# Cluster masks from cluster numbers through crossbar DMA transposes, in a routed-attention kernel with an expert router behind it

## The chip, the cores and the metric

The kernel runs on one core of one Trainium2 chip, in one launch. The metric is device time in microseconds (us), the median of the runs shown. Nothing is computed on the host.

## The reference: what is computed

The first half is attention that is restricted to clusters. Each query and each key is given to the centroid (16 for each head) with which it has the largest cosine, and a query sees only the keys of its own cluster:

```
q_assign = argmax(q_n @ c_n.T)          # 16 centroids for each head
k_assign = argmax(k_n @ c_n.T)
mask     = q_assign[..., :, None] == k_assign[..., None, :]
scores   = where(mask, scale * q @ k.T, -1e9)
attn     = softmax(scores);  out = attn @ v     # 4 batches, 8 heads, 768 rows, 64 columns
```

The second half takes the attention output as 3072 tokens of 512 values, gives each token to one of 8 experts by its cosine with the expert's embedding, and computes `gate * (relu(x @ w1[e]) @ w2[e])` with w1 of 512x1024 and w2 of 1024x512 for each expert. All is float32.

## The kernel before

**Tiling.** The attention is worked in 16 pairs: a pair is one batch and two heads (`pairs`), whose 2x64 columns fill 128 partitions. A pair has 12 units: two halves of the queries (`hq`, 384 columns each) times six blocks of 128 keys (`j`). Six units of the same half are a group, whose sums share one accumulator. For a unit, `scores` (L361) puts the scores transposed, keys on partitions, into a PSUM tile of two banks, one for each head; `expo` (L377) lets ScalarE (ACT) take the exponential into `prob`; `attend` (L382) multiplies it with v into `o_ps` and lets VectorE (DVE) add it to `acc`, the group's denominators before they are summed over partitions. `total` (L411) sums `acc` over partitions with a matmul, and DVE inverts it; `divide` (L427) scales the output; `rows` (L443) turns it back to rows.

**The mask.** It is added inside the score product. Each token has a one-hot row of its cluster, 16 columns and one column of +1 or -1, padded to 64 for each head; the product of the key's and the query's rows, the latter times 2**60, is 0 for the same cluster and -2**60 for another. So the first two matmuls of a unit (L369, bf16, K = 64 rows for each head) lay down the mask, and two float32 products add the scores.

**How a pair's masks are made** (`prep_pieces`, L238), one pair ahead of its use. `turn0` and `turn1` (L260) turn q and k, loaded in 32x32 blocks, with a DVE block transpose. `products` (L264): four matmuls with the centroids, copied out by ACT (`asT`, L276). `assign` (L278): three float32 transposes on TensorE (PE) bring tokens back on partitions (L281), DVE takes the maximum and compares (L289, L290), GpSimd (POOL) multiplies with 16 ... 1 so that ties go to the first cluster (L291). `choose` (L293): DVE's maximum `pm` (L297) is the cluster's number, and a compare with it writes the one-hot tile `oh` (L298). `turn_hot` (L305): 12 bf16 transposes on PE for q and k (L311), evicted by DVE as `qH` (L317) and by ACT as `kH` (L320). `values` (L323) adds up v on POOL, and `mean` (L332) turns that sum into a column `ev` that `divide` uses.

**The order of the work** is written out by hand for PE, DVE and ACT, which run their instructions in exactly the order of the program; POOL and SP (the queue that issues the loads) follow the order that the framework's scheduler chose. The main loop (L861) takes two units at a time; I call such a step an iteration, six of them (`it` 0 to 5) to a pair. In each, PE gets the scores of the *next* two units, then the pieces that `between` (L812) deals out, then the attend products of the present two units, and at `it` 0 and 3 the `total` of the group just finished:

```
it 0: turn1(n+1)      it 1: values, products(n+1), rows   it 2: assign(n+1), rows
it 3: choose(n+1)     it 4: hots(n+1)                     it 5: turn0(n+2)
```

Because scores run one iteration ahead, the first scores of pair n+1, and with them its masks, are asked for at the start of `it` 5 of pair n. The loads of v for pair n+1 are issued in `it` 0 and those of q and k for pair n+2 in `it` 1, all on SP. In pair 1 four loads of expert weights, 2 MB each, are issued as well (L870, L873). Pools: `prob` has five buffers (`pp`), `s_ps` two, the PSUM tile `misc` two, the masks two (`trp`).

**After the attention** (from about 408 us on) 28 blocks of 128 tokens go through the experts. The change touches nothing there.

Of the kernel before, what the change touches and what calls it, by code (L numbers as in the profile page):

```python
# [9 lines left out]
F32 = mybir.dt.float32  # L10
BF16 = mybir.dt.bfloat16
# [28 lines left out]
def kernel(  # L40
# [44 lines left out]
    w2s = [const.tile([P, KF, DM], F32, name=f"w2s{i}") for i in range(2)]  # L85

    ident = const.tile([P, P], F32, name="ident")
    identb = const.tile([P, P], BF16, name="identb")
    cnB = const.tile([P, NHP, 2 * C], F32, name="cnB")
    embT = const.tile([P, KD, 2 * C], F32, name="embT")  # L90
    prefc = const.tile([P, C], BF16, name="prefc")
# [74 lines left out]


    make_identity(nc, ident)
    make_identity(nc, identb)
    make_upper_triangular(nc, sltb, val=1.0, diag=False)  # L170
    nc.vector.memset(onesb, 1.0)
    nc.vector.memset(ones, 1.0)
# [22 lines left out]
    nc.vector.tensor_scalar(tok_t, tok_i, 6, None, ALU.arith_shift_right)  # L195
    nc.vector.tensor_scalar(tok_hi, tok_t, 1, None, ALU.add)

    ohs = [const.tile([P, NJ // 2, 4, 2, D], BF16, name=f"oh{i}") for i in range(2)]
    for oh in ohs:
        nc.gpsimd.memset(oh, 0.0)  # L200
        for t in range(2):
            nc.gpsimd.memset(oh[:, :, 2 * t : 2 * t + 2, :, C : C + 1], (-1.0, 1.0)[t])

    def unit_rows(dst, src, n):

# [32 lines left out]
    def prep_pieces(n):  # L238

        hp = pairs[n][1]  # L240
        t = ld[n]
        oh = ohs[n % 2]

        def turn(nm, half):
            if half == 0:
# [18 lines left out]
        def products():  # L264

            bk = misc()
            for i in range(4):
                nc.tensor.matmul(  # L268
                    bk[2 * C * i : 2 * C * i + 2 * C, 0:HS],
                    lhsT=cnB[:, hp],  # L270
                    rhs=t["qk"[i // 2] + "T"][:, HS * (i % 2) : HS * (i % 2) + HS],
                    start=True,
                    stop=True,
                )
            t["asT"] = smp.tile([P, HS], F32, tag="asT", name="asT", bufs=1)
            nc.scalar.copy(t["asT"], bk[:, 0:HS])  # L276

        def assign():  # L278
            bk = misc()
            for u in range(NJ // 2):  # L280
                nc.tensor.transpose(  # L281
                    bk[:, P * u : P * u + P], t["asT"][:, P * u : P * u + P], ident
                )
            shp = [P, 4 * NJ, C]
            asn = bk[:, 0 : 4 * NJ * C].rearrange("p (g c) -> p g c", c=C)
            amax = smp.tile(shp[0:2], F32, tag="amax", name="amax")
            sel = smp.tile(shp, BF16, tag="sel", name="sel", bufs=1)
            t["sel"] = sel
            nc.vector.tensor_reduce(amax, asn, axis=AXX, op=ALU.max)  # L289
            nc.vector.tensor_tensor(sel, asn, bc(amax, shp, 2), ALU.is_equal)  # L290
            nc.gpsimd.tensor_tensor(sel, sel, bc(prefc, shp, 1), ALU.mult)  # L291

        def choose():  # L293

            shp = [P, 4 * NJ, C]
            pm = smp.tile(shp[0:2], BF16, tag="pm", name="pm")
            nc.vector.tensor_reduce(pm, t["sel"], axis=AXX, op=ALU.max)  # L297
            nc.vector.tensor_tensor(  # L298
                oh.rearrange("p u t h c -> p (u t h) c")[:, :, 0:C],
                t["sel"],  # L300
                bc(pm, shp, 2),
                ALU.is_equal,
            )

        def turn_hot(i, nm):  # L305
            hot = t[nm + "H"] = trp.tile([P, S], BF16, tag=nm + "H", name=nm + "H")
            bank = misc()
            bk = bank.bitcast(BF16)
            for j in range(NJ):
                half, u = divmod(j, NJ // 2)  # L310
                nc.tensor.transpose(  # L311
                    bk[:, P * j : P * j + P],
                    oh[:, u, 2 * i + half].rearrange("p h c -> p (h c)"),
                    identb,
                )
            if nm == "q":
                nc.vector.tensor_scalar(hot, bk[:, 0:S], BIG, None, ALU.mult)  # L317
            else:
                mean(bank)
                nc.scalar.copy(hot, bk[:, 0:S])  # L320
                nc.vector.tensor_copy(t["ev"], bank[:, HS : HS + 1])

        def values():  # L323

# [7 lines left out]
        def mean(bk):  # L332

            nc.tensor.matmul(
                bk[:, HS : HS + 1],
                lhsT=t["vs"][:, 0].rearrange("p h d -> p (h d)"),
                rhs=epsc,
                start=True,
                stop=True,
            )  # L340
            t["ev"] = smp.tile([P, 1], F32, tag="ev", name="ev")

        return {
            "turn0": lambda: turn_blocks("q") if n else (turn("q", 0), turn("k", 0)),
# [2 lines left out]
            "products": products,  # L347
            "assign": assign,
            "choose": choose,
            "hots": lambda: (turn_hot(0, "q"), turn_hot(1, "k")),  # L350
        }


# [7 lines left out]
    def scores(i):  # L361

        n, hq, j = units[i]
        t = ld[n]
        s_ps = un[i]["s_ps"] = psS.tile([P, 2, 512], F32, tag="s_ps", name="s_ps")
        for l, r, first in (("kH", "qH", True), ("kT", "qT", False)):
            for h in range(2):
                rows = slice(D * h, D * h + D)
                nc.tensor.matmul(  # L369
                    s_ps[:, h, 0:HS],  # L370
                    lhsT=t[l][rows, P * j : P * j + P],
                    rhs=t[r][rows, HS * hq : HS * hq + HS],
                    start=first,
                    stop=not first,
                )

    def expo(i):  # L377
# [4 lines left out]
    def attend(i):  # L382

        n, hq, j = units[i]
        d, g = un[i], gr[i // GU]
        if j == 0:
            g["o_ps"] = psO.tile([P, 512], F32, tag="o_ps", name="o_ps")
        for h in range(2):
            nc.tensor.matmul(  # L389
                g["o_ps"][D * h : D * h + D, 0:HS],  # L390
                lhsT=ld[n]["v"][:, j, h],
                rhs=d["prob"][:, h],
                start=(j == 0),
                stop=(j == NJ - 1),
            )
        if j == 1:
            g["acc"] = xp.tile([P, 2, HS], F32, tag="acc", name="acc")
            nc.vector.scalar_tensor_tensor(  # L398
                out=g["acc"],
                in0=un[i - 1]["prob"],  # L400
                scalar=NJ * EPS,
                in1=d["prob"],
                op0=ALU.add,
                op1=ALU.add,
            )
            un[i - 1].clear()
        elif j > 1:
            nc.vector.tensor_tensor(g["acc"], g["acc"], d["prob"], ALU.add)  # L408
            d.clear()

    def total(g):  # L411

        d = gr[g]
        bk = misc()
        for h in range(2):
            nc.tensor.matmul(  # L416
                bk[D * h : D * h + D, 0:HS],
# [385 lines left out]
        (3, 3): lambda: (pa.tokens(), fetch(0), fetch(1), fetch(2)),  # L803
    }

    def piece(n, name):
        if n < NP:
            if n not in prepare:
                prepare[n] = prep_pieces(n)
            prepare[n][name]()  # L810

    def between(n, it):  # L812
        b, nb = divmod(n, NHP)
# [16 lines left out]
                rows(2 * n - 1)  # L830
        elif it == 3:
            piece(n + 1, "choose")
        elif it == 4:
            piece(n + 1, "hots")
        if b > 0:
            if nb == 0 and it == 3:
                route[b - 1] = route_pieces(b - 1)
# [14 lines left out]
            weights(1)  # L852

    with tc.manual_schedule(engines={EngineType.PE, EngineType.DVE, EngineType.Activation}):
        for name in ("turn0", "turn1", "values", "products", "assign", "choose", "hots"):
            piece(0, name)
        load(1, "qk")
        for m in range(2):
# [150 lines left out]
```

## Time and profile before

| | |
|---|---|
| median of three runs | 842.67 us (839.86 to 843.57) |
| the profiled execution | 841.56 us, its span 839.8 us |
| attention stage, first scores to last attend product | 21.95 to 407.9 us |
| one pair, from one v load's issue to the next (190.46 to 213.74) | 23.3 us |
| mean of the 12 pairs from 71.85 to 358.6 us | 23.9 us |
| VectorE busy between 180 and 210 us | 26.35 of 30 us |
| ScalarE, GpSimd in the same 30 us | 17.13 and 3.76 us |

The span is the time between the first and the last instruction on the core, and the 1.8 us between it and the execution's own time lie outside of the records. The page shows busy time for each engine; a busy PE means that matmuls overlap without a hole, each with its pipeline's fill and drain in its duration, so what a matmul costs is read from the distance between starts. "PEld" is the load of stationary weights, "SPq" the issue of a DMA on the SP queue. A group's line names the tile that is written, an arrow, and the tiles that are read.

### The profile page before, as it was taken

What the parts mean: (1) busy time and instruction counts of PE and PEld (TensorE: products, weight loads), DVE (VectorE), ACT (ScalarE), POOL (GpSimd) and SP (SyncE); (2) the same over time, 40 slices, a digit from 0 to 9 for tenths busy, and PEclk for the clock granted to TensorE, in tenths of its full rate; (3) what the DMA queues carried; (4) which work ended last, traced back from release to release, by engine and by line L of the source; (5) the groups of instructions that cost most, each with busy time, mean ns of one, the idle gap of its engine ahead of it and who ended that gap; (6) DMA issues with size and microseconds to landing.
All of it is one profiled execution on the core that took longest, in us unless ns stands there. A gap on an engine that the chain in (4) does not pass through costs nothing.

```text
span 839.8 us, 12523 instructions
## 1 busy us (share of the span) xinstructions
PE 806.9 (96%) x5047; PEld 474.3 (56%) x5047; DVE 372.1 (44%) x521; ACT 293.9 (35%) x459; POOL 126.9 (15%) x172
## 2 busy tenths in 40 slices
PE   4999999999999999998997999999999999999995
PEld 2444444444444444443685667676776768676672
DVE  3588888898889988898560000000000000000000
ACT  2555556755576556754431111111111111111110
POOL 4011110211111111220120111110101011010100
PEclk9999999999999999999998999999999999999998
DMA  9269552284343721040279449566574838126400
GB/s 156 97 242 182 71 62 43 26 132 57 57 58 73 116 47 23 9 95 1 74 169 396 152 146 334 205 220 252 183 289 155 315 130 328 43 93 249 157 29 22
DMA packets 158381, 115.23 MB, mean 137 GB/s; under 512 B 124261, under 2 KB 124261, under 8 KB 158320
## 3 DMA queue, kind: packets, MB, share of 16 engines
q1 hardware_dynamic: 153664, 100.69, 44.8%
q0 software_dynamic: 4480, 13.65, 4.3%
q8 instruction: 42, 0.69, 0.3%
q14 instruction: 19, 0.16, 0.1%
q10 hardware_dynamic: 176, 0.05, 0.0%
HBM read 152.11 MB, written 13.64 MB: 197 GB/s over the span
## 4 chain that ended last, share of the span: by engine, by line
PE 45%; issue 27%; DMA 23%; DVE 2%; SPq 1%; POOL 1%; ACT 0%; POOLq 0%; DVEq 0%
PE s_ps L369 18%; DMA out_dram<-y,sidx 18%; PE o_ps L389 15%; PE misc L416 2%; DMA w1s<-in_moe_w_dram 2%; DMA out_dram<-y,gidx 2%; PE h_ps L753 2%; PE misc L450 2%; PE misc L268 1%; PE misc L311 1%; PE misc L281 1%; SPq L154 1%; PE y_ps L769 1%; DMA q<-in_q_dram 1%; PE misc L472 1%
## 5 line engine op out<-in xcount | busy, mean ns | idle before, releaser
L753 PEld LDWEIGHTS h_ps<-xTm,w1s 128*128 128x128 f32 x1792 | 204.7, 194 | 28.4 <-DVE xTm L741 17.5
L753 PE MATMUL h_ps<-xTm,w1s 128*128 128x128 f32 x1792 | 210.2, 278 | 7.0 <-DMA w1s<-in_moe_w_dram 7.0
L769 PE MATMUL y_ps<-w2s,hT 128*128 128x512 f32 x448 | 201.1, 592 | 0.0
L380 ACT ACTIVATE prob<-s_ps 128x768 f32<-128x768 f32 x192 | 153.8, 810 | 121.0 <-PE s_ps L369 112.7
L741 DVE COPY xTm<-x_ps 128x512 f32<-128x512 f32 x24 | 16.6, 692 | 332.1 <-PE x_ps L739 332.1
L369 PE MATMUL s_ps<-qT,kT 64*128 64x384 f32 x768 | 157.6, 489 | 0.0
L389 PE MATMUL o_ps<-prob,v 128*64 128x384 f32 x768 | 145.1, 499 | 0.0
L408 DVE TENSOR_TENSOR acc<-acc,prob 128x768 f32<-128x768 f32 x128 | 129.4, 1011 | 3.5
L769 PEld LDWEIGHTS y_ps<-w2s,hT 128*128 128x128 f32 x448 | 81.0, 190 | 81.8 <-issue 81.8
L760 ACT ACTIVATE hT<-h_ps 128x512 f32<-128x512 f32 x56 | 33.4, 597 | 207.7 <-PE h_ps L753 207.7
L425 DVE RECIPROCAL den<-den 128x384 f32<-128x384 f32 x32 | 81.6, 2551 | 27.2 <-ACT den L424 27.2
L389 PEld LDWEIGHTS o_ps<-prob,v 128*64 128x64 f32 x768 | 46.6, 136 | 64.9 <-issue 56.9
L369 PEld LDWEIGHTS s_ps<-qT,kT 64*128 64x128 f32 x768 | 69.9, 192 | 22.1 <-issue 22.1
L779 ACT ACTIVATE y<-y_ps,xin 128x512 f32<-128x512 f32 x28 | 19.2, 687 | 150.3 <-PE y_ps L769 139.1
L780 POOL DMA_INDIRECT out_dram<-y,sidx x24 | 24.0, 1000 | 291.2 <-ACT y L779 285.3
L369 PE MATMUL s_ps<-qH,kH 64*128 64x384 bf16 x384 | 64.4, 332 | 1.0 <-ACT kH L320 0.9
L369 PEld LDWEIGHTS <-kH 64*128 64x128 bf16 x384 | 19.0, 94 | 71.6 <-issue 48.9
L327 POOL TENSOR_TENSOR vs<-v 128x384 f32<-128x384 f32 x16 | 16.8, 1049 | 198.7 <-DMA v<-in_v_dram 158.6
L291 POOL TENSOR_TENSOR sel<-sel,prefc 128x384 bf16<-128x384 bf16 x16 | 24.2, 1516 | 91.5 <-DVE sel L290 91.5
L709 POOL DMA_INDIRECT xin<-x_rows,gidx x28 | 29.7, 1059 | 41.1 <-issue 19.7
L398 DVE SCALAR_TENSOR_TENSOR acc<-prob 128x768 f32<-128x768 f32 x32 | 30.0, 936 | 3.1 <-ACT prob L380 3.1
L416 PE MATMUL misc<-acc,ones 128*64 128x384 f32 x128 | 26.6, 493 | 3.0 <-DVE acc L408 3.0
(185 smaller groups left out, 437.4 us busy)
## 6 DMA issues: line engine op xcount, KB each, us to landing
w1s<-in_moe_w_dram SPq DMA_DIRECT2D x30, 2048.0 KB
w2s<-in_moe_w_dram SPq DMA_DIRECT2D x30, 2048.0 KB
x_rows<-xr SPq DMA_DIRECT2D x4, 1539.0 KB
v<-in_v_dram SPq DMA_DIRECT2D x32, 192.0 KB
q<-in_q_dram SPq DMA_DIRECT2D x60, 96.0 KB
k<-in_k_dram SPq DMA_DIRECT2D x60, 96.0 KB
xin<-x_rows,gidx POOLq DMA_INDIRECT x28, 7.2
q<-in_q_dram SPq DMA_DIRECT2D x2, 192.0 KB
```

The costliest lines, as they stand in the source:

```text
L291: nc.gpsimd.tensor_tensor(sel, sel, bc(prefc, shp, 1), ALU.mult)
L369: nc.tensor.matmul(s_ps[:, h, 0:HS], lhsT=t[l][rows, P * j : P * j + P], rhs=t[r][rows, HS * hq : HS * hq + HS], start=first, stop=not first,)
L380: nc.scalar.activation(d["prob"], d["s_ps"][:, :, 0:HS], ACTF.Exp, scale=scale)
L389: nc.tensor.matmul(g["o_ps"][D * h : D * h + D, 0:HS], lhsT=ld[n]["v"][:, j, h], rhs=d["prob"][:, h], start=(j == 0), stop=(j == NJ - 1),)
L398: nc.vector.scalar_tensor_tensor(out=g["acc"], in0=un[i - 1]["prob"], scalar=NJ * EPS, in1=d["prob"], op0=ALU.add, op1=ALU.add,)
L408: nc.vector.tensor_tensor(g["acc"], g["acc"], d["prob"], ALU.add)
L416: nc.tensor.matmul(bk[D * h : D * h + D, 0:HS], lhsT=ones, rhs=d["acc"][:, h], start=True, stop=True,)
L425: nc.vector.reciprocal(d["den"], d["den"])
L709: nc.gpsimd.indirect_dma_start(out=xin, out_offset=None, in_=x_rows[0:n], in_offset=bass.IndirectOffsetOnAxis(ap=gidxs[part][:, c : c + 1] ...
L753: nc.tensor.matmul(bk[:, m : m + P], lhsT=w1s[j % 2][:, c, f0 + m : f0 + m + P], rhs=d["xT"][:, P * c : P * c + P], start=(c == 0), stop=( ...
L760: nc.scalar.activation(d["hT"][:, f0 : f0 + 512], bk, ACTF.Relu)
L769: nc.tensor.matmul(bk, lhsT=d["hT"][:, P * c : P * c + P], rhs=w2s[j % 2][:, c], start=(c == 0), stop=(c == KF - 1),)
```

## The change

The one-hot tile and its 12 PE transposes go. In their place each token carries three numbers, its cluster number c, c squared and a constant, so that the product of a key's and a query's three numbers is a constant times (cq - ck) squared. The parts, as the diff has them:

- `products` no longer lets ACT copy the bank; DVE turns it in 32x32 blocks out of PSUM into `asn`. `assign` reads `asn` in SBUF, and its three PE transposes are gone.
- `choose`: after `pm`, POOL writes `cd` (32 tokens by 1536 columns for each of four partition groups; 64 columns for each head of which three are used) with three small operations, and four DMA transposes write the mask tile `hot` (128 by 4 by 384), two of them for the two halves of q, two for those of k. They are issued on SP, for the first pair on ACT's queue. There is one `cd`, where there were two one-hot tiles.
- `hots` is gone from `it` 4. `mean` moves into `total`, in the same PSUM bank, at the end of `it` 3.
- `attend`: at `j` = 1 POOL adds the first two `prob` tiles into `two`; at `j` = 2 DVE adds `two`, the epsilon and the third `prob` (the fused operation that stood at `j` = 1). DVE has one addition fewer for each group.

In the changed kernel's program the four transposes of pair n+1 stand on SP behind the v loads of that pair and most of the q and k loads of pair n+2, in pair 1 behind the four weight loads and all of the q and k loads. On POOL, between the tie-breaking multiply and the three operations on `cd`, stands the `two` of the group that begins at `it` 3. The first scores of a pair wait for the transposes of q's first half, of k's first half, and, being in one queue, of what lies between.

```diff
-    ohs = [const.tile([P, NJ // 2, 4, 2, D], BF16, name=f"oh{i}") for i in range(2)]
-    for oh in ohs:
-        nc.gpsimd.memset(oh, 0.0)
...
+    cd = const.tile([P, S // (2 * SQ), 2, D], BF16, name="cd")
+    wcd = const.tile([P, S // SQ], BF16, name="wcd")
+    nc.gpsimd.memset(cd, 0.0)
+    for i, (p0, w, c) in enumerate(((0, -BIG, BIG / 2), (D, -2.0, 1.0))):
+        g = slice(p0, p0 + D)
+        nc.gpsimd.memset(wcd[g], w)
+        nc.gpsimd.memset(cd[g, :, :, 2 - 2 * i : 3 - 2 * i], c)
...
-            t["asT"] = smp.tile([P, HS], F32, tag="asT", name="asT", bufs=1)
-            nc.scalar.copy(t["asT"], bk[:, 0:HS])
+            t["asn"] = smp.tile([P, HS], F32, tag="asn", name="asn", bufs=1)
+            nc.vector.transpose(t["asn"], bk[:, 0:HS])
 
         def assign():
-            bk = misc()
-            for u in range(NJ // 2):
-                nc.tensor.transpose(
-                    bk[:, P * u : P * u + P], t["asT"][:, P * u : P * u + P], ident
-                )
...
-            nc.vector.tensor_tensor(
-                oh.rearrange("p u t h c -> p (u t h) c")[:, :, 0:C],
-                t["sel"],
-                bc(pm, shp, 2),
-                ALU.is_equal,
-            )
-
-        def turn_hot(i, nm):
...
-            for j in range(NJ):
-                half, u = divmod(j, NJ // 2)
-                nc.tensor.transpose(
...
-            if nm == "q":
-                nc.vector.tensor_scalar(hot, bk[:, 0:S], BIG, None, ALU.mult)
-            else:
-                mean(bank)
-                nc.scalar.copy(hot, bk[:, 0:S])
-                nc.vector.tensor_copy(t["ev"], bank[:, HS : HS + 1])
+            pm, w = (x.rearrange("p (s h) -> p s h", h=2) for x in (pm, wcd))
+            nc.gpsimd.tensor_tensor(cd[..., 1], pm, w, ALU.mult)
+            for i, p0 in enumerate((0, D)):
+                g = slice(p0, p0 + D)
+                nc.gpsimd.tensor_tensor(cd[g, :, :, 2 * i], pm[g], cd[g, :, :, 1], ALU.mult)
+            t["H"] = trp.tile([P, 4, HS], BF16, tag="hot", name="hot")
+            for i in range(4):
+                (nc.sync if n else nc.scalar).dma_start_transpose(
+                    out=t["H"][:, i].rearrange("r (s t) -> r s t", t=SQ),
+                    in_=cd[SQ * i : SQ * i + SQ].rearrange("p s h c -> p (s h c)"),
+                )
...
             t["ev"] = smp.tile([P, 1], F32, tag="ev", name="ev")
+            nc.vector.tensor_copy(t["ev"], bk[:, HS : HS + 1])
...
         if j == 1:
+            d["two"] = xp.tile([P, 2, HS], F32, tag="two", name="two", bufs=1)
+            nc.gpsimd.tensor_tensor(d["two"], un[i - 1]["prob"], d["prob"], ALU.add)
+            un[i - 1].clear()
+        elif j == 2:
             g["acc"] = xp.tile([P, 2, HS], F32, tag="acc", name="acc")
             nc.vector.scalar_tensor_tensor(
                 out=g["acc"],
-                in0=un[i - 1]["prob"],
+                in0=un[i - 1]["two"],
...
-        elif j > 1:
+        elif j > 2:
             nc.vector.tensor_tensor(g["acc"], g["acc"], d["prob"], ALU.add)
...
         bk = misc()
+        if g % 2 == 0:
+            piece(units[GU * g][0] + 1, "mean", bk)
...
-        elif it == 4:
-            piece(n + 1, "hots")
+        elif it == 4 and n == 0:
+            piece(0, "mean", misc())
```

## The prediction

> **What bounds the kernel now.** I read the page's busy times first, then the busy times of 30 us stretches, then the timelines of PE, DVE and POOL over one pair.
>
> ```profile
> 180.00:210.00 30.00, 30.00 (x213) 13.80 (x209) 26.35 (x30) 17.13 (x24) 3.76 (x5) 1.00 0.55 64
> 210.00:240.00 30.00, 30.00 (x213) 13.03 (x209) 25.52 (x30) 17.82 (x29) 3.47 (x4) 1.00 0.26 45
> ```
>
> (PE, PE's weight loads, DVE, ACT, POOL, clock, DMA share, GB/s.) PE has no hole in the attention stage, DVE is at 85 to 88%, POOL at 12%. So PE's order of work is the bound, and each microsecond taken out of it counts, as long as nothing that it waits for becomes late. PE's timeline over `it` 2 (end) to `it` 5 of one pair:
>
> ```profile
> 200.20 0.55 PE L281 MATMUL misc<-ident,asT 128*128 128x128 f32 x3
> 200.58 0.49 PE L450 MATMUL misc<-ident,xT 128*128 128x128 f32 x3
> ...
> 202.45 0.34 PE L369 MATMUL s_ps<-qH,kH 64*128 64x384 bf16 x2
> ...
> 207.98 0.84 PE L311 MATMUL misc<-identb,oh 128*128 128x128 bf16 x12
> 208.66 0.34 PE L334 MATMUL misc<-epsc,vs 128*128 128x1 f32 x2
> 208.92 1.51 PE L389 MATMUL o_ps<-prob,v 128*64 128x384 f32 x8
> 210.36 0.34 PE L369 MATMUL s_ps<-qH,kH 64*128 64x384 bf16 x2
> ```
>
> From start to start the three transposes of L281 take 200.58 - 200.20 = 0.38 us, the twelve of L311 208.66 - 207.98 = 0.68, `mean` 0.26. `it` 3 begins at 202.45, `it` 5, where the next pair's masks are first read, at 210.36. What makes the masks (DVE's rows, then POOL's):
>
> ```profile
> 202.90 1.48 DVE L408 TENSOR_TENSOR acc<-acc,prob 128x768 f32<-128x768 f32 x1
> 204.31 0.54 DVE L297 TENSOR_REDUCE pm<-sel 128x24 bf16<-128x384 bf16 x1
> 204.88 0.56 DVE L298 TENSOR_TENSOR oh<-sel,pm 128x384 bf16<-128x384 bf16 x1
> ```
> ```profile
> 202.01 1.56 POOL L291 TENSOR_TENSOR sel<-sel,prefc 128x384 bf16<-128x384 bf16 x1 [5.28 <-DVE sel L290]
> ```
>
> `pm` is there at 204.85, 2.4 us after `it` 3 began. An addition beside POOL's L291 takes 1.48 us in place of the usual 0.97.
>
> One more place shows what a wait of PE costs, near the end of the stage:
>
> ```profile
> 386.67 1.18 PE L416 MATMUL misc<-acc,ones 128*64 128x384 f32 x4 [2.17 <-DVE acc L408]
> 387.79 0.50 PE L369 MATMUL s_ps<-qH,kH 64*128 64x384 bf16 x2
> 388.08 1.49 PE L369 MATMUL s_ps<-qT,kT 64*128 64x384 f32 x4
> ```
>
> After 2.17 us of idleness the same four matmuls take 1.49 us that take 0.81 elsewhere. From 386.67 to 390.83 PE does what takes 0.74 + 1.72 = 2.46 us in the pair above (205.51 to 206.25, 206.25 to 207.98): a further 1.7 us lost.
>
> **What the Trainium skill says.** (1) "TensorE: Matmul & The Clock Gate", Part 1: PE falls to half its clock after an idle window of some 3.4 us and needs as long to recover. The trace agrees on the slow stretch (some 4 us), but here 2.17 us of idleness was enough. (2) "SBUF — State Buffer", Who interferes with whom: a DVE instruction with two SBUF inputs and a GpSimd instruction that reads SBUF exclude each other for a whole instruction. The trace agrees: 1.48 for 0.97 above, and L291 took 0.91 us alone at the start (at 16.89). (3) "VectorE: DVE Perf Modes", The three transpose paths: a crossbar DMA transpose of 128x128 bf16 is given as 1309 ns. (4) "DMA: Bandwidth & Descriptors", Latency and other measured facts: a fixed cost near 2 us, most of it the receipt of the last bytes, less for targets other than HBM. No crossbar transfer is in this trace; the nearest to (4) is the first load of centroids, issued at 0.75, read by ACT at 3.50, so at most 2.75 us.
>
> **The change part by part**, against the profiled execution's 841.6 us (the median of the runs is 1.1 us above it).
>
> *PE's transposes go*: 0.38 + 0.68 = 1.06 us a pair. Pairs 1 to 15 are prepared beside PE's stream: 15 x 1.06 = -15.9 us. `mean` costs the same 0.26 in its new place; its sum of v was ready at 196.7, 9 us before.
>
> *ACT* loses `asT` (0.48 us) and `kH` (0.80) a pair. ACT waits for PE's scores anyway: nothing.
>
> *DVE* loses `oh` 0.56, `qH` 0.50 and two first additions (2 x 0.94), and gains the transpose of 384 columns out of PSUM, at 0.56 from the nearest row (`amax`, the same read). About 2.4 us less of 21 a pair; DVE isn't the bound, so nothing in the steady pairs. Where it was, at 386.67, it is earlier by one addition for each group; I take 3 of the 2.17 + 1.7 us there as gained: -3.
>
> *POOL's `two`*: 128 columns take 0.45 us and 384 take 1.00 (L328, L327), so 768 take 1.8. Twice a pair, 3.6 us on an engine that is busy for 3; its cost is what stands behind it. In POOL's order the `two` of `it` 3 stands between L291 and the three operations on `cd`. By (2) it shuts out, or is shut out by, DVE's second addition (L408). I take it as getting in after that addition: from 1.9 to 3.7 us after `it` 3's begin. Then three small ones: a chain of six eight-column additions (L514) took 2.23 us, 0.37 each; so 3 x 0.37 = 1.1, and `cd` is ready at 4.8, its first part at 4.5. Bounds: 3.5 if `two` costs nothing, 5.5 if it gets in first and delays `pm`.
>
> *The crossbar transposes*: three must land before `it` 5. That begins 210.36 - 202.45 = 7.9 us after `it` 3 before, less L311's 0.68 = 7.2 after (`mean` only moves). They start at some 4.7. The unknown is the time of one, 96 KB each. Below: the loads of q, k and v in 190 to 200 us are 7680 packets (6144 of 128 B, 1536 of 256 B) at shares 0.47 + 1.18 + 1.51 + 1.36 + 0.06 of 2 us of 16 engines, 19 ns a packet; if a transpose moves 256-byte rows, 384 packets, that is 0.5 us. As 64-byte runs, 1536 packets: 1.8. By (3), three times 128x128: 3.9. I take 0.9 each, near the lower end since sixteen engines share it, and 1.5 us from the last packet to PE: 4.7 + 2.7 + 1.5 = 8.9. **PE then waits 8.9 - 7.2 = 1.7 us in each pair.** Nothing shortens this in the next pair: the chain to `cd` starts from PE's own `total` at `it` 0, which is as late as PE is. Pairs 1 and 3 to 15, 14 of them: 14 x 1.7 = +24. The slow clock after a wait near 2 us costs up to 1.7 more; I take half, since 0.82 us of idleness (before L416 at 74.59) left it at full speed: 14 x 0.85 = +12. Behind the transposes on SP stands only part of k's loads for the pair after, needed 5 us later or more: nothing.
>
> *Pair 2* stands behind four weight loads:
>
> ```profile
> 51.30 17.10 SPq L154 DMA_DIRECT2D q<-in_q_dram  x4
> 68.50 3.24 SPq L154 DMA_DIRECT2D k<-in_k_dram  x4
> ```
>
> These loads are issued only by 71.74, and the transposes come after: landing near 71.7 + 2.7 + 1.5 = 76, where `it` 5 begins at 67: 9 us, and 1.7 for the clock, less 1.05 us (0.23 + 0.82) for which PE stands still there now: +9.
>
> *The first pair*: `asT` and L281 go (the maximum some 1.1 us earlier), and `cd` (1.1) plus three transposes (4.2) stand where L311, `qH`/`kH` took 19.27 to 21.95, less `oh` 0.56: +1.
>
> Sum: -15.9 - 3 + 24 + 12 + 9 + 1 = +27; 841.6 + 27 + 1.1 = **870 us**.
>
> **The rivals.**
> *A, the transposes land in time* (0.4 us each, 1.2 to land: 4.7 + 2.4 = 7.1). Then PE's gain stays: -15.9 - 3 + 1 + 6 for pair 2 = -12: 830 us, faster. For it: the queue is empty from 200 on (share 0.00 in the stretches to 214), SP waits for nothing else. It decides at 0.8 us per transpose with its landing spread over three, that is 2.5 us in all after `cd`. Against: the fixed cost alone nearly uses that up.
> *B, a short wait*, 0.6 us each and 1.3 to land, 7.8: 0.6 x 14 = +8, no slow clock: -15.9 - 3 + 8 + 9 + 1 = -1: 842, no change.
> *C, the crossbar is slow*, 2.5 us each: 4.7 + 7.5 + 1.5 = 13.7, a wait of 6.5 and the slow clock 1.7: 14 x 8.2 = 115; -18.9 + 115 + 13 = +109: 952. For it: the price under (3) scaled by size would be slower still.
> *D, VectorE becomes the bound* through the lock: 21 - 2.4 + 2 x 1.8 = 22.2 us a pair, against PE's 23.3 - 1.06 = 22.2. It would take back the rest of the gain at most: the time is then B's.
>
> **How the numbers follow.** My forecast 0.47 (its own range, with one transpose at 0.7 to 1.3 us, 848 to 905), A 0.23, B and D together 0.12, C 0.18. The range runs from A's middle to C's: 828 to 948. Half a percent, 4 us, is about what a measurement of this kernel can tell from no change. Faster 0.24 (A and a little of B), same 0.09, slower 0.67.
>
> **What would show it.** In PE's timeline after, the bf16 scores of the first unit of each pair carry a wait for a DMA of `hot`, of about 1.7 us, fourteen times, and the float32 scores behind it last 1.5 us in part of the pairs. In POOL's timeline `two` lies between `sel` and the `cd` rows, which end some 4.8 us after `it` 3 begins. Pair 2 shows one wait near 9 us. If PE's rows have no wait for `hot`, A is right and I am wrong; if the wait is over 4 us, C. If PE waits for `acc` and DVE has no idle time, D.

## The result and the profile after

The changed kernel takes 864.11 us (860.88 to 869.56, four runs) against 842.46 us of the kernel before (839.86 to 843.57, four runs): the ratio is 1.0268, with a 95% interval of 1.0208 to 1.0328. The forecast was 870 us, slower, in a range of 828 to 948. The profiled execution took 860.88 us (its span is 859.0), 19.3 us more than the 841.56 of the one before.

The time went into the attention. Its last `total` starts at 432.95 us, before at 411.67: 21.3 us later. What follows, to the end of the span, is 2.1 us shorter (426.05 for 428.13), of which 1.4 are PE's wait for `w1s` (5.6 us for 7.0).

I show the views of the prediction again, now of the kernel after. The two stretches of 30 us (PE, PE's weight loads, DVE, ACT, POOL, clock, DMA share, GB/s):

```profile
180.00:210.00 30.00, 28.05 (x180) 11.59 (x180) 25.40 (x30) 14.34 (x21) 11.17 (x10) 1.00 0.74 122
210.00:240.00 30.00, 28.74 (x189) 11.74 (x187) 23.20 (x23) 14.43 (x21) 10.76 (x12) 1.00 0.50 79
```

PE, which had no hole, is now idle for 1.95 and 1.26 us. POOL works for 11 us instead of 3.5. DVE is idle for longer than before, so VectorE did not become the bound.

PE's timeline from the start of `it` 3 (195.24) to the first masks of the next pair (204.63):

```profile
195.24 0.34 PE L357 MATMUL s_ps<-hot 64*128 64x384 bf16 x2
...
198.40 0.38 PE L316 MATMUL misc<-epsc,vs 128*128 128x1 f32 x2
199.04 0.87 PE L407 MATMUL misc<-acc,ones 128*64 128x384 f32 x4 [0.25 <-DVE ev L324]
...
201.55 1.51 PE L373 MATMUL o_ps<-prob,v 128*64 128x384 f32 x8
204.63 0.34 PE L357 MATMUL s_ps<-hot 64*128 64x384 bf16 x2 [1.57 <-DMA hot<-cd]
204.81 0.81 PE L357 MATMUL s_ps<-qT,kT 64*128 64x384 f32 x4
```

There is the forecast wait for a DMA of `hot`. The float32 scores behind it take 0.81 us, so the clock did not fall. There is also a wait that the prediction did not have: `total` (L407) waits for DVE's copy `ev`. What makes the masks, on POOL, SP and DVE:

```profile
194.28 1.56 POOL L287 TENSOR_TENSOR sel<-sel,prefc 128x384 bf16<-128x384 bf16 x1 [3.74 <-DVE sel L286]
195.81 2.54 POOL L382 TENSOR_TENSOR two<-prob 128x768 f32<-128x768 f32 x1
198.29 0.31 POOL L294 TENSOR_TENSOR cd<-pm,wcd 128x24 bf16<-128x24 bf16 x1
198.68 0.68 POOL L297 TENSOR_TENSOR cd<-pm,cd 64x24 bf16<-64x24 bf16 x2
```
```profile
194.12 2.54 DVE L397 TENSOR_TENSOR acc<-acc,prob 128x768 f32<-128x768 f32 x2
196.58 0.54 DVE L292 TENSOR_REDUCE pm<-sel 128x24 bf16<-128x384 bf16 x1
198.82 0.16 DVE L324 COPY ev<-misc 128x1 f32<-128x1 f32 x1 [1.70 <-PE misc L316]
```
```profile
199.00 5.64 SPq L300 DMA_TRANSPOSE hot<-cd  x4
...
223.41 5.11 SPq L300 DMA_TRANSPOSE hot<-cd  x4
```

`pm` is done at 197.1, but POOL is still at `two`, so the first `cd` operation starts 1.2 us later. `two` takes 1.81 us where nothing disturbs it; here it takes 2.54, because an addition of DVE got in first, which ends at 196.66. Then SP needs 5.11 us for the four transposes where nothing disturbs it, 1.28 for each; the issue of one lasts 1.25 us in the median of 60. PE waits for three. In the set at 199.00 one of them took 1.79 us. In the undisturbed set at 223.41 the third issue ends at 227.2, and PE starts at 228.49, 1.3 us later.

Pair 2, on PE and on SP:

```profile
81.01 0.50 PE L357 MATMUL s_ps<-hot 64*128 64x384 bf16 x2 [11.73 <-DMA hot<-cd]
81.30 1.49 PE L357 MATMUL s_ps<-qT,kT 64*128 64x384 f32 x4
```
```profile
55.94 17.54 SPq L153 DMA_DIRECT2D q<-in_q_dram  x4
73.57 2.18 SPq L153 DMA_DIRECT2D k<-in_k_dram  x4
75.85 5.11 SPq L300 DMA_TRANSPOSE hot<-cd  x4
```

The loads of q and k hold SP until 75.75, and the transposes come after. This wait alone is 11.73 us, and the slow clock behind it 1.8.

The late place near the end of the attention:

```profile
407.95 0.87 PE L407 MATMUL misc<-acc,ones 128*64 128x384 f32 x4 [3.15 <-DVE acc L397]
```
```profile
401.76 1.81 POOL L382 TENSOR_TENSOR two<-prob 128x768 f32<-128x768 f32 x1 [8.12 <-ACT prob L364]
```
```profile
401.94 1.80 DVE L627 TENSOR_TENSOR wa<-wa,eq 128x144 f32<-128x144 f32 x1
```

In the kernel before the same operation of DVE was:

```profile
382.21 0.31 DVE L636 TENSOR_TENSOR wa<-wa,eq 128x144 f32<-128x144 f32 x1
```

The wait there was 2.17 us. It grew, since DVE's small routing operation takes 1.80 us in place of 0.31: it stands beside POOL's `two`, and ends 0.17 us after it.

**Where the 21.3 us are.** I take the distance from one `total` to the next in both traces. The first `total` comes 1.9 us later (the first pair waits for its transposes). The stretch with pair 2's wait is 11.7 us longer, the late place 1.0. The other 28 stretches, two for each of 14 pairs, are 6.7 us longer, 0.48 a pair. In a pair PE has lost 1.06 us of transposes, `mean` costs 0.54 more than before (below), and the 14 waits for `hot` sum to 10.6 us (0 to 1.57 us, mean 0.76). That makes 0.24 of the 0.48; the rest are in part waits for `acc` (named in two stretches, at 259.29 and 356.39, which are 0.4 us longer than mere arithmetic gives: 10.54 for 11.08 - 0.68 - 0.26 = 10.14).

### The profile page after: what moved, and what is told of

Its sections match the earlier page's. It is cut to its first block, busy times and chain, and to the rows that moved or that the text cites. A ratio compares the mean times of both kernels' runs of the same rounds, so it can differ in the third digit from the quotient of the medians.

```text
span 859.0 us, 12213 instructions
## 1 busy us (share of the span) xinstructions
PE 795.8 (93%) x4807; PEld 455.9 (53%) x4807; DVE 355.2 (41%) x473; ACT 274.1 (32%) x427; POOL 208.0 (24%) x249
## 4 chain that ended last, share of the span: by engine, by line
issue 28%; PE 25%; DMA 24%; DVE 12%; SPq 4%; POOL 4%; ACT 2%; ACTq 0%; POOLq 0%; DVEq 0%
DMA out_dram<-y,sidx 17%; PE s_ps L357 10%; PE o_ps L373 7%; DVE den L416 4%; DVE acc L397 3%; DMA hot<-cd 3%; SPq L300 2%; POOL two L382 2%; PE misc L407 2%; DMA w1s<-in_moe_w_dram 2%; DMA out_dram<-y,gidx 2%; PE h_ps L744 2%; SPq L153 1%; DVE acc L386 1%; PE misc L441 1%
## 5 line engine op out<-in xcount | busy, mean ns | idle before, releaser
L397 DVE TENSOR_TENSOR acc<-acc,prob 128x768 f32<-128x768 f32 x96 | 116.9, 1218 | 4.6
L382 POOL TENSOR_TENSOR two<-prob 128x768 f32<-128x768 f32 x32 | 71.0, 2218 | 142.1 <-ACT prob L364 142.1
L357 PE MATMUL s_ps<-hot 64*128 64x384 bf16 x384 | 64.5, 332 | 32.5 <-DMA hot<-cd 32.4
L357 PEld LDWEIGHTS <-hot 64*128 64x128 bf16 x384 | 19.0, 94 | 104.6 <-issue 48.9
L407 PE MATMUL misc<-acc,ones 128*64 128x384 f32 x128 | 27.3, 504 | 7.7 <-DVE ev L324 3.8
L386 DVE SCALAR_TENSOR_TENSOR acc<-two,prob 128x768 f32<-128x768 f32 x32 | 30.4, 950 | 0.0
```

The costliest lines, as they stand in the source:

```text
L357: nc.tensor.matmul(s_ps[:, h, 0:HS], lhsT=l[rows], rhs=r[rows], start=first, stop=not first)
L382: nc.gpsimd.tensor_tensor(d["two"], un[i - 1]["prob"], d["prob"], ALU.add)
L386: nc.vector.scalar_tensor_tensor(out=g["acc"], in0=un[i - 1]["two"], scalar=NJ * EPS, in1=d["prob"], op0=ALU.add, op1=ALU.add,)
L407: nc.tensor.matmul(bk[D * h : D * h + D, 0:HS], lhsT=ones, rhs=d["acc"][:, h], start=True, stop=True,)
```

## The experiments

Each is timed beside runs of the kernel before on the same chip. That is 839.29 us for experiments 1 to 4, so the changed kernel's ratio puts it at about 862 there, and the ratio's interval allows 857 to 867: each difference from the changed kernel below is uncertain by some 5 us, and I give what the profiled executions show beside it. The kernel before took 841.08 for 5, 6 and 7; 840.89 for 8, 9 and 10; 841.07 for 11 and 12.

My theory after the result: a pair's length is set by one chain, which begins and ends on PE: the last masks, the `total`s, DVE's `sel`, POOL's `sel`, `two` and `cd`, three issues on SP, the landing. Whatever shortens the chain should gain, and whatever shortens PE's work alongside it should not. Rivals were VectorE and the lock (D of the prediction), the data of the transposes in place of their issue, and a mere sum of PE's waits.

### 1. The order of the transposes

```diff
-            for i in range(4):
+            for i in (0, 2, 3, 1):
```

The first scores need q's first half (0) and k's first half (2). In the changed order two issues stand in PE's way, not three.

> The four transposes of a pair are issued in the order q's first half, k's first half, k's second half, q's second half, so the first scores of a pair stand behind two transposes and not three. If PE waits for the third issue on SP (1.27 us each, from start to start), the waits for hot (10.6 us over the 14 pairs other than the first two late ones, 0.27 to 1.57 each) all but vanish and pair 2's 11.73 us falls by 1.3: about 853 us. If the transposes land together whatever their order (the crossbar or the receipt is what is late), or if something else of the chain takes its place, the time stays at 862 to 866 us.

Measured: 853.33 us, ratio 1.0169 (1.0150 to 1.0189), 8.5 us less than the changed kernel; the last `total` starts 7.2 us earlier (425.75 for 432.95), of which 1.6 come from the first pair, whose transposes on ACT's queue are in the new order too. In the steady pairs only two waits for `hot` are left, of 0.57 us each. One of them:

```profile
195.51 0.87 PE L407 MATMUL misc<-acc,ones 128*64 128x384 f32 x4 [0.25 <-DVE ev L324]
...
200.11 0.34 PE L357 MATMUL s_ps<-hot 64*128 64x384 bf16 x2 [0.57 <-DMA hot<-cd]
```

The third transpose was the wait. Pair 2's wait fell only from 11.73 to 11.41 us, not by the 1.3 expected: PE came there 2.2 us earlier, the transposes only 1.2. In eleven pairs a smaller one, 0.19 to 0.35 us for `acc` at `total`, came into view, so not all of what was gained at the masks was kept. `mean`'s 0.25 us stays.

### 2. The weight loads spread out

One of the four 2 MB loads in each of the pairs 1 to 4, at `it` 4, in place of all in pair 1 (the same loads, also in the kernels below where it says "spread").

```diff
-            if it == 0 and n == 1:
...
+            if it == 4 and 1 <= n <= 4:
+                dst = (w1s, w2s)[(n - 1) % 2][(n - 1) // 2]
+                src = (moe_w1, moe_w2)[(n - 1) % 2][0]
+                nc.sync.dma_start(out=dst, in_=src.rearrange("(c p) f -> p c f", p=P))
```

> The four 2 MB weight loads of pair 1 are spread, one in each of pairs 1 to 4. If pair 2's wait of 11.73 us comes from the transposes standing behind them in SP's queue, it falls to about 1 us, and the slow clock behind it (1.8 us) goes: 864 - 12 = 852 us. If a single weight load ahead of the transposes still delays each of pairs 2 to 5 by some 3 us, the gain is near nothing: 862 us.

Measured: 850.43 us, 1.0144 (1.0122 to 1.0165), 11.4 us less; the last `total` starts 12.3 us earlier. Pair 2's wait is 1.03 us, like that of any other pair, and the others stay:

```profile
70.25 0.34 PE L357 MATMUL s_ps<-hot 64*128 64x384 bf16 x2 [1.03 <-DMA hot<-cd]
```

A rival is that the weights, 8 MB on the way, slowed the transposes themselves. The changed kernel's trace speaks against it: in pair 2 PE starts 1.36 us after the third issue ends, in the other pairs 1.27 to 1.38. So it was the queue on SP.

### 3. `mean` back in `it` 4

```diff
-        if g % 2 == 0:
-            piece(units[GU * g][0] + 1, "mean", bk)
...
+            piece(n + 1, "mean", misc())
```

The last line stands in `between` at `it` 4; `mean` has a bank of its own again.

> The matmul of the column ev goes back to iteration 4 and to a PSUM bank of its own, so total no longer waits for DVE to read ev. That wait costs PE 0.54 us a pair, 8 us in all. If the chain from total at iteration 0 through DVE, GpSimd and SP to the third transpose sets the pair's length, PE only comes earlier to its wait for hot, which grows by about as much: the time stays within 2 us of 864. If PE's own work sets it, 8 us less: 856 us.

Measured: 860.87 us, 1.0261 (1.0234 to 1.0289): within 1 us of the changed kernel; the last `total` starts 1.8 us later. PE's wait for `ev` is gone, but PE's waits for `hot`, those of the first pair and of pair 2 included, sum to 42.1 us instead of 32.4. The gain was taken back at the next wait: PE reaches the masks earlier, the masks don't come earlier. After three waits of the steady pairs PE's products are now slow, as here:

```profile
206.13 0.50 PE L357 MATMUL s_ps<-hot 64*128 64x384 bf16 x2 [2.51 <-DMA hot<-cd]
206.43 1.49 PE L357 MATMUL s_ps<-qT,kT 64*128 64x384 f32 x4
```

### 4. The first addition back on VectorE

```diff
-            nc.gpsimd.tensor_tensor(d["two"], un[i - 1]["prob"], d["prob"], ALU.add)
...
-                in0=un[i - 1]["two"],
+                in0=un[i - 1]["prob"],
```

`j` = 1 and up are as in the kernel before.

> A group's first addition goes back to DVE, the rest of the change stays. If GpSimd's addition (2.5 us, of which 0.7 is waiting for DVE) delays the numbers that the transposes read, these start 2 to 2.5 us earlier and the waits for hot go, pair 2's excepted: 864 - 10 = 854 us, and the wait near the end of the stage for DVE's additions (3.15 us) goes back to near 2. If DVE's relief by 0.94 us a group is worth more than that, because DVE is what PE waits for, it is slower: 870 us or more.

Measured: 855.87 us, 1.0202 (1.0185 to 1.0220), 6 us less; the last `total` starts 4.8 us earlier. Of the steady pairs' waits for `hot` 6.2 us are left of 10.6. With two additions more for VectorE in each pair, PE still waits for no `acc` in the steady pairs (three of its waits for `ev` are 0.71 us in place of 0.25), so VectorE's work is not the bound; the 870 us that rival D would give did not come. What its lock costs is another matter (experiments 7 and 12). The chain shortens by less than the whole of `two`, since `cd`'s first operation now waits itself beside DVE's addition (0.94 us for 0.31).

### 5. One transfer for both halves of q

```diff
-            for i in range(4):
+            for p0, m, o in ((0, D, 0), (D, SQ, 2), (D + SQ, SQ, 3)):
...
+                    in_=cd[p0 : p0 + m].rearrange("p s h c -> p (s h c)"),
```

Nothing else is undone. The masks of q are then read with a stride.

> The changed kernel, but with q's two halves turned by one transfer of 64 partitions (12 blocks of 128 columns) and k's halves by one each: three transfers in place of four, the one for q twice the size; the bf16 product reads q's rows with a stride. Two of them stand in the way, with the data of three. If each transfer costs SP some 1.25 us of issue whatever its size, as I believe, the issue of the first one lasts about 1.3 us and the time is that of the changed order, about 853. If the cost goes with the data, the first one lasts about 2.5 us and nothing is gained: 860 to 864. A strided read of q that PE dislikes would show in the bf16 scores (0.34 us from start to start of a pair of them) and could hide a gain.

Measured: 855.03 us, 1.0172 (1.0140 to 1.0204), the same as experiment 1 within the intervals. SP's row for a set of three:

```profile
99.40 3.98 SPq L300 DMA_TRANSPOSE hot<-cd  x3
```

Three transfers, one of twice the size, take 3.98 us, four of one size 5.11. The issue of the double one, which is the first, lasts 1.23 us in the median, and the next starts 1.33 us after it. So the price is by the transfer, not by the data, at these two sizes. A bf16 product takes 335 ns on the mean for 332, so the stride costs nothing that can be seen.

### 6. Order, loads and `mean` together

The edits of 1, 2 and 3, with the additions on GpSimd.

> The changed kernel with three of its costs taken away together: the transposes issued in the order q's first half, k's first half, k's second, q's second; the four weight loads one each in pairs 1 to 4; mean back in iteration 4 in a bank of its own. My theory: with two transposes in the way in place of three, PE's wait for the masks is gone nearly everywhere, so that mean's wait of 0.54 us a pair, which was hidden behind it when mean was moved alone, now counts. Before 839.3, PE's products gone -15.9, first pair +1, small waits for VectorE's acc and the end stall +2 to 4: 827 to 833, faster than both kernels; the three single gains (8.5, 11.4, 1) would only give 841 if they simply added. Rival: the chain's other links set the length (VectorE behind GpSimd's lock); then waits for acc take the place of the waits for the masks and the time stays at 838 to 843.

Measured: 833.50 us, 0.9922 (0.9896 to 0.9949). It is faster than both kernels, half a microsecond above what I expected, and 30 us below the changed kernel (864 on this chip), where the three gains sum to 21. The medians alone can't show that the gains don't add, by the uncertainty above; the traces do: the last `total` starts at 403.40, 29.6 us earlier, where the three alone give 7.2 + 12.3 - 1.8 = 17.7. `mean`'s wait counts once PE no longer waits behind it.

### 7. The same, and the first addition on VectorE

> The kernel of the three edits together, and in addition a group's first addition back on VectorE, so that GpSimd does only the masks. My theory: the addition on GpSimd cost something only by its place ahead of cd and by the lock with VectorE; once the masks are in time it matters little: 826 to 833, within 3 us of the three edits alone, the end stall 1 to 2 us shorter, no waits for acc in the steady pairs unless VectorE with 23 us of work a pair falls behind. Rival: VectorE is the bound without GpSimd's help, since a pair is now only some 22.3 us long: then waits for acc in each pair, and 838 or more.

Measured: 824.64 us, 0.9814 (0.9788 to 0.9840). The gain over experiment 6 is 9 us, three times what I had allowed. In the profiled execution PE has no wait left in the steady pairs. One of these pairs, from `it` 3 to the masks, on PE and SP:

```profile
194.67 0.34 PE L357 MATMUL s_ps<-hot 64*128 64x384 bf16 x2
...
197.73 0.82 PE L400 MATMUL misc<-acc,ones 128*64 128x384 f32 x4
...
201.95 0.34 PE L357 MATMUL s_ps<-hot 64*128 64x384 bf16 x2
```
```profile
198.12 5.12 SPq L300 DMA_TRANSPOSE hot<-cd  x4
```

The transposes start 3.45 us after `it` 3, and two issues and the landing (2 x 1.28 + 1.3 = 3.9) end at about 7.3; `it` 5 begins at 7.28. It just fits. The two stretches of a pair take 10.44 and 11.87 us where they took 11.08 and 12.20: 0.97 less a pair, and 16.2 us over the attention. That is nearly the gain that the prediction reckoned with for PE (1.06 a pair). The difference of the medians is 16.4 us.

### 8. Experiment 7 with three transposes in the way

The order 0, 1, 2, 3 again; all else as in 7.

> The kernel with weight loads spread, mean back in iteration 4 and the first addition on VectorE, but with the transposes in the changed kernel's order, so that three and not two stand in PE's way. It asks whether the third transpose alone is worth more than GpSimd's addition once all else is mended. A transfer is issued 1.27 us after the one before it, so PE waits up to 1.3 us longer in each of 14 pairs than with the other order, which has some slack: my theory gives 10 to 18 us more than 824.6, so 835 to 843, with waits for the masks of 0.5 to 1.5 us in nearly every pair and a slow clock behind few of them. Rival: with GpSimd relieved the masks are early enough even with three, no waits, within 3 us of 824.6.

Measured: 839.77 us, 0.9991 (0.9974 to 1.0009), 15 us more. The waits are there again, in eleven of the pairs, 1.05 to 1.40 us but for one of 3.04:

```profile
93.01 0.34 PE L357 MATMUL s_ps<-hot 64*128 64x384 bf16 x2 [1.05 <-DMA hot<-cd]
```

The first pair has the old order too, and its first `total` comes 1.7 us later than in experiment 7; most of the rest lies in the waits. One issue of some 1.3 us more on the chain takes back all that the change can gain.

### 9. A control: the kernel before with its weight loads spread

> A control: the kernel before, with nothing but the four weight loads spread one each over pairs 1 to 4. In its profile PE has waits near that place of only 0.82 us, so at most 1 us is to be gained: 0 to -1 us against before. If the gain were 5 us or more, part of what the mended kernels win would not be the change's.

Measured: 838.14 us, 0.9965 (0.9955 to 0.9975), 2.8 us less; I had expected 0 to 1. Its trace has lost the wait of 0.82 us, 1.0 with what hung on it. Its first scores start 0.8 us earlier as well (21.16 for 21.95), but that may be chance: experiments 1, 6, 7 and 11 begin alike, and their first scores lie between 21.27 and 21.83. The rest I can't place. So some 3 of the 16 us of experiment 7 belong to the loads, 13.5 to the change.

### 10. and 11. The routing work near the end, one iteration later

```diff
-        (2, 5): lambda: pa.dest(),
-        (3, 0): lambda: (pa.hot_blocks(), pa.hot_rows(0, 3)),
-        (3, 1): lambda: pa.hot_rows(1, 3),
-        (3, 2): lambda: pa.hot_rows(2, 3),
+        (3, 0): lambda: pa.dest(),
+        (3, 1): lambda: (pa.hot_blocks(), pa.hot_rows(0, 3)),
+        (3, 2): lambda: (pa.hot_rows(1, 3), pa.hot_rows(2, 3)),
```

Both start from experiment 7. The first also had k's transposes of the first pair on SP.

> The kernel with all four edits, and the routing work that VectorE does near the end of the attention moved one iteration later (what stood in iteration 5 of pair 14 goes to iteration 0 of pair 15, what stood there to iteration 1, two pieces together in iteration 2). PE there waits 2.31 us for VectorE's acc. Theory: VectorE is late by the 2.9 us of that piece, so the wait goes and 2 to 2.5 us are gained: 822 to 823. Rival: the wait only moves to the next total or to the tokens' matmuls: no gain.

Measured: 827.66 us, 0.9839 (0.9823 to 0.9856). The first scores start at 24.18 us, since SP's transposes stood behind a load until 21.59.

> The kernel with all four edits and the routing work near the end one iteration later, and nothing else (the run before it also had, by oversight, k's transposes of the first pair on SP, where they came 1.4 us too late behind a wait: first scores at 24.18 in place of 21.27). From its trace: the wait of 2.31 us for acc is gone, and 1.70 us for xT with a slow clock behind it have come in its place, so I now expect next to nothing: 823.5 to 825; the first idea, a gain of 2 to 2.5 us, would give 822 to 822.6.

Measured, the work moved and nothing else: 826.29 us, 0.9835 (0.9820 to 0.9850): no gain over experiment 7, and 1.3 us above what I expected. The stretch of the late place is 2.5 us shorter, the next one 1.8 longer, with a wait of 1.71 us for `xT`. So the moved work gives 0.7 us in the trace, and the rival was right in the main: moving DVE's work moves the place where PE notices that DVE is late. The trace also has two waits for masks that experiment 7's has not, 1.67 and 0.89 us:

```profile
181.87 0.34 PE L357 MATMUL s_ps<-hot 64*128 64x384 bf16 x2 [1.67 <-DMA hot<-cd]
```

They lie 190 and 100 us ahead of what was edited, and the run before has them as well (1.63 and 0.58 us), so they are hardly the edit's. In all three traces one load of k holds SP for 5 to 9 us at both places, after the write of `x_rows`, as in the next experiment. At the first place it ended 0.6 us before the transposes began in experiment 7; here they began some 0.7 us late behind it, and the first one's issue took 2.30 us for 1.34. So these waits are in some traces and not in others, and they hide what the moved work gives.

### 12. GpSimd's addition in one group only

Experiment 6, with `two` only in the group that begins at `it` 0, where nothing of the masks is behind it.

```diff
-        if j == 1:
+        if j == 1 and hq == 0:
             d["two"] = xp.tile([P, 2, HS], F32, tag="two", name="two", bufs=1)
...
```

> The kernel with the three edits (833.5 with GpSimd's addition in both groups of a pair, 824.6 with none on GpSimd), with GpSimd's addition only in the group that begins at iteration 0, where it stands behind nothing of the masks; the group that begins at iteration 3, whose addition stands ahead of cd, is added by VectorE alone. If the 9 us that the addition costs come from its place ahead of cd, they go: 824 to 826. If each addition costs the same, by the lock with VectorE, half stays: 828 to 830.

Measured: 835.29 us, 0.9931 (0.9915 to 0.9947), not different from experiment 6. Both expectations were wrong. The trace says why. In experiment 6 PE is held up in each pair by about 0.3 us, by the masks or by `acc`, whichever is later. Taking `two` from in front of `cd` frees the masks; but the other `two`, which stays, runs into DVE's last additions of the group before:

```profile
234.09 1.81 POOL L382 TENSOR_TENSOR two<-prob 128x768 f32<-128x768 f32 x1 [7.89 <-ACT prob L364]
```
```profile
234.28 3.50 DVE L397 TENSOR_TENSOR acc<-acc,prob 128x768 f32<-128x768 f32 x2
```
```profile
237.83 0.87 PE L405 MATMUL misc<-acc,ones 128*64 128x384 f32 x4 [0.19 <-DVE acc L397]
```

Two additions of DVE take 3.50 us for 1.94 and end at 237.8, and `total` starts 0.36 us later than with them in time (10.80 us from `total` to `total` for 10.44). This is the lock of "SBUF — State Buffer", Who interferes with whom, in the Trainium skill. It costs some 5 us over the attention; 1.5 more at the late place, in experiment 12 a slow clock there too, 2.7 us that experiment 6 has not. And in two pairs a load holds up the transposes, after the write of `x_rows`; PE waits 3.13 and 1.64 us. The second:

```profile
267.40 7.75 SPq L153 DMA_DIRECT2D k<-in_k_dram  x1
275.25 5.24 SPq L300 DMA_TRANSPOSE hot<-cd  x4
```

`cd` was ready at 273.8; SP was still at the issue of one load of k. The masks have next to no slack even in experiment 7, so whatever is late on this queue is paid for at once.

## Why the prediction was right, point by point

The forecast, slower by a short wait for the masks in each pair, is what happened, and 864.11 lies 6 us under 870. Not all of its terms held.

- *PE's transposes go, -15.9 us*: right in the main; experiment 7, which has nothing else in its way, shows 0.97 a pair, 14.6 us.
- *`mean` costs the same 0.26 in its new place*: this failed. PE's order there is `mean`, `total`; `mean`'s column lies in the bank that `total` writes, so `total` waits for DVE to copy the column out; in a bank of its own (experiment 3) the wait is gone. The stretch that holds `mean` should be 0.38 us shorter without L281, and is 0.42 longer: `mean` with its wait costs 0.80. That is 0.54 a pair, 8 us, by a wait that I hadn't looked for: I had costed the moved instruction, not who stands behind it. It did not show in the time either, since PE would only have waited later (experiment 3).
- *`cd` is ready at 4.8 us after `it` 3*: it was there sooner, at 4.1 (199.36 - 195.24), with the transposes' issue beginning at 3.76. The three operations run at 0.3 to 0.35 us, and `sel` and `two` come earlier.
- *The transposes, 0.9 us each and 1.5 to land*: the size failed, 1.28 and 1.3. So did the reason: I shared bytes over sixteen engines, but the distance from one transpose to the next is the time of its issue on SP.
- *They land at 8.9 and are wanted at 7.2*: in the pair of 223.41 `it` 3 began at 219.66 (`mean` at 222.82 less 3.16), the masks are used at 228.49, and would have been at 227.48. So 8.83 and 7.82. The landing was right by two errors that cancel, the deadline later by what `mean`'s wait adds. The wait is 1.01 there, 0.76 on the mean: 10.6 us in place of 24.
- *The slow clock, +12*: 0 in the steady pairs, where no wait passed 1.57 us. With the waits, which came out 13 us smaller, this is the largest miss of the sum; half of 1.7 in each pair was a guess between two observations.
- *Pair 2, +9*: the mechanism right, the size 11.73 + 1.8 - 1.05 = 12.5. I had the loads end at 71.74 as before; they ended at 75.75, since SP came to them 4.6 us later (55.94 for 51.30). Of the 1.05 us that I took off, the trace of before shows 0.82 as a wait; the 0.23 isn't in it, though the stretch was 1.0 us longer than its like.
- *The first pair, +1*: 1.9 us.
- *The late place, -3*: failed in sign, +1.0. I took it that DVE has one addition fewer, and did not look at what POOL does at that moment: `two` holds up DVE's small operation for 1.5 us.
- *Rivals*: A, B and C asked the right question, how long a transpose takes. A's time, 830, is nearly reached (833.5, experiment 6) when three things are mended: how many issues stand in the way and what else is on the queue, both of which could be seen before, and `mean`. D's bound didn't come: DVE is idle for longer than before. Its lock did, at other places: with the addition on POOL, experiment 6 is 9 us slower than experiment 7.

In sum: the terms that were too large (slow clock -12, waits -13) and those missed or too small (`mean` +8, the late place +4, pair 2 +3.5, the first pair +1, the rest of the steady stretches, in part waits for `acc`, +3) leave about -6: some 21 us over the attention where 27 were forecast, and it is 21.3 us longer. What follows is 2.1 us shorter, for which the forecast had no term. The direction and its cause, a short wait for the masks in each pair, were foreseen; that 864 came so near 870 is in part luck, since misses of 25 us one way and 19 the other cancelled.

**A faster version.** Experiment 7 takes 824.64 us, 1.9% less than the kernel before: crossbar masks, two issues in the way, the weight loads spread, `mean` in its own bank, all additions on VectorE. The change's idea for PE was sound; its helpers, the addition on GpSimd and the shared bank, the order of four lines, and what else stood on their queue cost more than it gains.

**What stays open.** About 1 us of experiment 9's gain. How long PE may stand still before its clock falls (below). Why one load of k holds SP for so long after the write of `x_rows`.

## What to carry to other kernels

When work leaves the engine that is the bound, write down the chain that must now be in time, from the last thing that engine gives it to the first thing it takes back, with the issues on the queue one by one, and order them by who is wanted first. If several waits lie on the same stretch, only the one that ends last costs: mending one shows nothing or little (`mean` 1 us alone, one of the two additions none), and their gains don't add up (8.5 + 11.4 + 1 alone, 30 together). An operation on GpSimd is not free merely because GpSimd is idle: ask what VectorE does in the same microseconds, and who waits for that.

## What the runs showed of the hardware

- The issue of a DMA transpose of 32 partitions by 1536 columns of bf16 holds SP for 1.25 us in the median of the changed kernel (1.19 to 1.95, 60 of them), one of 64 partitions for 1.23 (experiment 5); on ACT's queue four took 5.27 us. In the changed kernel PE uses the data 1.27 to 1.38 us after the last issue that it needs has ended; in experiments 3 and 8 this was in some pairs up to 3.05.
- A load of 96 KB whose issue takes about 0.6 us held SP for 7.75 us (experiment 12) soon after the 1.5 MB write of `x_rows` was issued, and everything behind it on the queue waited. In experiments 6, 7, 10 and 11 such a load held it for 5 to 9 us.
- VectorE's operations with two inputs were held up beside GpSimd's addition of two tiles: 1.80 us for 0.31 in the changed kernel, 3.50 for 1.94 in experiment 12.
- The clock. "TensorE: Matmul & The Clock Gate", Part 1, in the Trainium skill gives an idle window of some 3.4 us. Here waits of 1.97 us (experiment 4), 2.16, 2.51 and 2.52 (experiment 3), 2.16 (experiment 9) and 3.04 (experiment 8) were followed by products at about half speed, 1.1 to 1.5 us for 0.81. Waits of 1.93 us (experiment 3), 2.31 (experiment 7), 3.13 (experiment 12) and 3.71 (experiment 6) were not. So the length of a wait alone doesn't decide it between 1.97 and 3.71 us, and what does, these runs don't show. The longest wait that left the clock alone:

```profile
379.94 0.87 PE L405 MATMUL misc<-acc,ones 128*64 128x384 f32 x4 [3.71 <-DVE acc L397]
380.74 0.34 PE L357 MATMUL s_ps<-hot 64*128 64x384 bf16 x2
380.91 0.81 PE L357 MATMUL s_ps<-qT,kT 64*128 64x384 f32 x4
```

The shortest that didn't, 1.97 us before 204.02:

```profile
204.84 0.33 PE L357 MATMUL s_ps<-hot 64*128 64x384 bf16 x2
205.00 1.14 PE L357 MATMUL s_ps<-qT,kT 64*128 64x384 f32 x4
206.07 2.83 PE L373 MATMUL o_ps<-prob,v 128*64 128x384 f32 x8
```
